# Eleven transfers of six partitions in place of half a block of wo

## The chip, the cores and the metric

The kernel runs on one core of a Trainium2 chip. The metric is device time in microseconds (us) of one execution. All inputs lie in the chip's memory (HBM) and are brought by DMA into SBUF, which has 128 partitions; a core's DMAs are carried by 16 DMA engines, told apart from the compute engines TensorE (PE; PEld for its weight loads), VectorE (DVE), ScalarE (ACT), GpSimd (POOL) and SyncE (SP). SP computes nothing here: it issues nearly all DMAs.

## The reference, cut to what matters

One decode step of a transformer block: attention over a key and a value cache, and a small MLP. B = 4 sequences, one new token each, H = 32 heads, Sk = 4096 cached positions, Dh = 128, D = 640, F = 1728, all bfloat16.

```python
q = (layernorm(x) @ wq)                     # (4, 640) @ (640, 4096), split into 32 heads
scores = einsum("bhqd,bhkd->bhqk", q, k_cache) * Dh ** -0.5
p = softmax(scores)
o = einsum("bhqk,bhkd->bhqd", p, v_cache)
h = x + o.reshape(4, 4096) @ wo             # wo: (4096, 640)
out = h + mlp(layernorm(h))                 # (640, 1728), an activation, (1728, 640)
```

The two caches have 4 * 32 * 4096 * 128 elements each, 134.2 MB; wo has 5.2 MB.

## The kernel before, in words

**Groups.** The 32 heads and 4 sequences are walked in NG = 32 groups, `g = 0..31`: a group is G = 4 heads (`hq = g // 4`) of one sequence (`b = g % 4`). The key tile `kt` of a group is `[128, 128, 128]`: a partition holds 128 positions of one head, 32 KB, so that 128 partitions hold four heads of 4096 positions. One DMA of 4 MB brings it; `vt`, the value tile, is alike. There are two buffers of each.

**A group's work.** DVE multiplies `kt` by the broadcast query (line 367, in four parts), PE sums over the head's dimension by matmuls with the identity (line 374), DVE ends that sum (line 386), the softmax follows (lines 393 to 425), and in the next group PE multiplies the probabilities by `vt` (line 257).

**Order of the DMAs.** It is written out by hand (`manual_schedule`): instructions run on each engine in the order of the program, and every DMA but the load of x goes through SP. At the end of group `g` SP issues `kt` of group g + 2 (when the buffer that group g used is free), then `vt` of group g + 1. In groups 8 to 11, after these two, it issues two blocks of wo each. The loads that follow the last group's are those of the MLP's weights (lines 501 to 507). The last `vt` (group 31) comes in four quarters, the last `kt` in two halves.

**wo.** The tile `wo_sb` is `[128, 32, 640]`; a block is 4 of its 32 rows `h`, 640 KB, 128 partitions with 5120 contiguous bytes each (in the last block, four times 1280 bytes). The eight blocks are read by `project(hq)` (line 344), block `hq` by `project(hq)`, at the end of groups 14, 15, 16, 17, 22, 26 and 30 (`PROJ_AT`) and once after the loop. Block 5, which is `h = 20..23`, is read in group 26. `wo_sb` takes the memory that wq had.

**What the prediction's steps touch.** `load_kv` (line 92; DMAs at line 100), the loop over groups (line 427), the loads of wo (line 471), the load of b1 (line 476, one partition), the load of x (line 110, four partitions, by ACT), the store of the output (line 649, 20 partitions), `pv_moving` (line 254).

The calls of lines 449 to 474, with the diff, show the order in which a group ends:

```python
        if g + 2 < NG:
            kts[g + 2] = load_k(g + 2)
        if 1 <= g < NG - 1:
            pv_moving(g - 1, 0, R)
            pv_copy(g - 1)
            vts.pop(g - 1)
        if g in PROJ_AT:
            project(PROJ_AT[g])
        if g + 1 < NG:
            vts[g + 1] = load_v(g + 1)
        ...
        if g in WO_AT:
            ...
```

Of the kernel before, what the change touches and what calls it, by code (L numbers as in the profile page):

```python
# [16 lines left out]
def kernel(  # L17
# [24 lines left out]
    nc = tc.nc  # L42

    B, Sq, D = A_x.shape
    _, H, Sk, Dh = A_k_cache.shape
# [3 lines left out]
    G = 4  # L49
# [5 lines left out]
    HQ = H // G  # L55
# [47 lines left out]
    def load_k(g):  # L103
        return load_kv(kpool, "kt", A_k_cache, g, NP)

    def load_v(g):
        return load_kv(vpool, "vt", A_v_cache, g, VP)
# [35 lines left out]
    for q in range(G):  # L143
        nc.vector.tensor_copy(
            out=sel[:, :, q, q * PH : (q + 1) * PH],
            in_=ident[0:N, 0:N].unsqueeze(2).to_broadcast([N, N, PH]),
# [81 lines left out]
    for hq in Q_AT[-1]:  # L228
# [12 lines left out]
        out=pick[:, :],  # L241
        in_=ident_f[:, :].rearrange("p (t i) -> p i t", t=T)[:, 0 : J * G, :],
# [11 lines left out]
    def pv_moving(g, r0, r1):  # L254
        for r in range(r0, r1, J):
            c0 = 128 // T * (r // J % T)
            nc.tensor.matmul(  # L257
                p_ps[c0 : c0 + J * G, :],
                lhsT=e2[g % NE2][:, r : r + J, :].rearrange("p j q -> p (j q)"),
                rhs=vts[g][:, r : r + J, :].rearrange("p j d -> p (j d)"),  # L260
                start=(r < J * T),
                stop=(r >= r1 - J * T),
            )

    def pv_copy(g):
        blocks[g] = work.tile([128, J * Dh], FP32, tag="p_sb", bufs=1, name=f"p_sb{g}")
        nc.scalar.copy(out=blocks[g][:, :], in_=p_ps[:, :])  # L267

    def add_blocks(g, stop=True):
        o = ot_of(g)  # L270
        p_sb = blocks.pop(g)
        for j in range(J):
            nc.tensor.matmul(  # L273
                o,
                lhsT=p_sb[:, j * Dh : (j + 1) * Dh],
                rhs=pick[:, j * G : (j + 1) * G],
                start=(j == 0),
                stop=(stop and j == J - 1),
            )
        return o  # L280
# [13 lines left out]
    def row_sums(hq):  # L294
        l_ps = ps.tile([128, N, G], FP32, tag="small")
        nc.tensor.matmul(  # L296
            l_ps[:, :, :],
            lhsT=ones_f[:, :],
            rhs=rs2[:, hq * N : (hq + 1) * N, :],
            start=True,  # L300
            stop=True,
        )
        rls[hq] = work.tile([128, N, G], FP32, tag="rl", name=f"rl{hq}")
        nc.vector.reciprocal(out=rls[hq][:, :, :], in_=l_ps[:, :, :])  # L304

    def normalise(hq):
        nc.vector.tensor_tensor(
            out=otn[:, hq, :, :],
            in0=ot.pop(hq)[:, :, :],
            in1=rls.pop(hq)[:, :, :],  # L310
            op=ALU.mult,
        )
# [15 lines left out]
    def regroup(hq):  # L328
        o4_ps = ps.tile([128, G, N], FP32, tag="small", name=f"o4_{hq}")
        for q in range(G):  # L330
            for i in range(G):
                nc.tensor.matmul(  # L332
                    o4_ps[q * PH : (q + 1) * PH, i, :],
                    lhsT=ident4[:, i, :],
                    rhs=otn[:, hq, :, q],
                    start=True,
                    stop=True,
                )
        nc.scalar.copy(out=o4[:, hq, :, :], in_=o4_ps[:, :, :])

    yT = ps.tile([128, DC, N], FP32, tag="yT")
    wo_sb = []

    def project(hq):

        for h in range(hq * G, (hq + 1) * G):
            for c in range(DC):
                nc.tensor.matmul(
                    yT[:, c, :],
                    lhsT=wo_sb[0][:, h, c * 128 : (c + 1) * 128],  # L350
                    rhs=o4[:, hq, h % G, :] if hq < HQ - 1 else otn[:, hq, :, h % G],
                    start=(h == 0 and c == 0),
                    stop=(h == H - 1 and c == DC - 1),
                )
# [3 lines left out]
    def mul_and_sum(g, part):  # L358

        hq, b = divmod(g, N)  # L360
        r0 = part * RP
        kt = kts[g][:, r0 : r0 + RP, :]
        s_ps = ps.tile([128, RP, W], FP32, tag="s", bufs=2, name=f"s{g}_{part}")
        s_of[g, part] = s_ps
        for k in range(NQ):
            d0 = k * DQ
            nc.vector.tensor_tensor(  # L367
                out=kt[:, :, d0 : d0 + DQ],
                in0=kt[:, :, d0 : d0 + DQ],
                in1=qbs[:, hq, b, d0 : d0 + DQ].unsqueeze(1).to_broadcast([128, RP, DQ]),  # L370
                op=ALU.mult,
            )
            for d in range(d0, d0 + DQ, W):
                nc.tensor.matmul(  # L374
                    s_ps[:, :, :],
                    lhsT=ident[:, :],
                    rhs=kt[:, :, d : d + W],
                    start=(d == 0),
                    stop=(d == Dh - W),
                )  # L380
            yield

    def finish_sum(g, part):
        if part == 0:
            s_sbs[g] = work.tile([128, R], FP32, tag="s_sb", name=f"s_sb{g}")
        nc.vector.tensor_reduce(  # L386
            out=s_sbs[g][:, part * RP : (part + 1) * RP],
            in_=s_of.pop((g, part))[:, :, :],
            axis=AX.X,
            op=ALU.add,  # L390
        )
# [35 lines left out]
    for g in range(NG):  # L427
        hq, b = divmod(g, N)
        for part in range(NP):
            now = mul_and_sum(g, part)  # L430
            before = None
            next(now)
            if part > 0:
                finish_sum(g, part - 1)
                if g >= 2:
                    add_blocks(g - 2)
                    if b == 1:
                        row_sums(hq - 1)
                        normalise(hq - 1)
                if g in PROJ_AT:  # L440
                    regroup(PROJ_AT[g])
            elif g >= 1:
                finish_sum(g - 1, NP - 1)
                before = softmax(g - 1)
                next(before)
            next(now)
            if before is not None:
                next(before)
        kts.pop(g)
# [10 lines that stand above are left out]
        for n in Q_AT.get(g, ()):  # L460
            q_chunk(n)
            q_broadcast(n)
        if g in WO_AT:

            if not wo_sb:
                wo_sb.append(wbig.tile([128, H, D], BF16, tag="w", name="wo_sb"))
            h0 = WO_AT[g] * WOC
            for h in range(h0, h0 + WOC, G):

                order = "(p i) n -> p i n" if h + G < H else "(i p) n -> p i n"  # L470
                nc.sync.dma_start(
                    out=wo_sb[0][:, h : h + G, :],
                    in_=A_wo[h * Dh : (h + G) * Dh, :].rearrange(order, i=G),
                )
            if WO_AT[g] == 0:
                nc.sync.dma_start(out=b1_row[:, :], in_=B_b1.rearrange("(o f) -> o f", o=1))
        if g == B1_AT:
            b_ps = ps.tile([128, FC], FP32, tag="small", name="b_ps")
            for c in range(FC):
                cols, fw = f_chunk(b1_row[:, :], c)  # L480
                nc.tensor.matmul(
                    b_ps[0:fw, c : c + 1],
                    lhsT=cols,
                    rhs=ident[0:1, 0:1],
                    start=True,
                    stop=True,
                )
            nc.vector.tensor_copy(out=b1T[:, 0:C2], in_=b_ps[:, 0:C2])
            nc.vector.tensor_copy(out=b1T[0:FREM, C2:FC], in_=b_ps[0:FREM, C2:FC])
# [56 lines left out]
    for dst in (h2T, hc):  # L546
        nc.vector.tensor_tensor(
            out=dst[:, :, :],
# [10 lines left out]
    for c0, c1 in W1_PARTS:  # L559
        for c in (0, C2, *range(1, C2)):  # L560
# [9 lines left out]
            if c0 == 0 and c == 4:  # L570
# [3 lines left out]
                    out=std[:, :], in_=v_ps[:, :], func=ACT.Sqrt, bias=eps_t[:, :], scale=1.0  # L574
# [5 lines left out]
        out=h1n[:, :, :],  # L580
# [6 lines left out]
        out=h1s[:, :, :],  # L587
# [9 lines left out]
        out=tb[:, :, :],  # L597
# [8 lines left out]
        out=ta[:, :, :], in0=tb[:, :, :], scalar1=-0.5, scalar2=-1.0, op0=ALU.mult, op1=ALU.add  # L606
# [4 lines left out]
        out=act_t[:, :, :],  # L611
# [10 lines left out]
    for i, (w2, c) in enumerate(w2_of):  # L622
        rows = 128 if c < C2 else FREM
# [10 lines left out]
        out=oT[:, :, :].rearrange("p n c -> p c n"),  # L634
# [46 lines left out]
```

## Time and profile before

| what | value |
|---|---|
| median of three runs | 667.99 us (667.97 to 668.5) |
| the profiled execution's own time | 668.62 us |
| its span, first to last instruction | 666.8 us |
| bytes moved by DMA | 283.81 MB, mean 426 GB/s |
| share of the 16 DMA engines' time that the data's queue took | 98.9% |
| busy: PE, DVE, ACT, POOL | 444.7, 353.4, 115.0, 2.4 us |
| mean granted TensorE clock | 0.837 of full speed |

The profile is of one execution. The span leaves out 1.8 us of that execution's time, which lie before the first and after the last instruction, and the execution took 0.63 us longer than the median of the runs. A queue's share is the time that its packets took, as a share of the time of 16 DMA engines over the span. A packet is what one DMA engine moves in one piece; here it is one partition's contiguous bytes, 32768 in a `kt` or `vt`. The trace keeps of each packet its queue, start, duration and size, but not which of the 16 DMA engines carried it.

### The profile page before, as it was taken

What the parts mean: (1) busy time and instruction counts of PE and PEld (TensorE: products, weight loads), DVE (VectorE), ACT (ScalarE), POOL (GpSimd) and SP (SyncE); (2) the same over time, 40 slices, a digit from 0 to 9 for tenths busy, and PEclk for the clock granted to TensorE, in tenths of its full rate; (3) what the DMA queues carried; (4) which work ended last, traced back from release to release, by engine and by line L of the source; (5) the groups of instructions that cost most, each with busy time, mean ns of one, the idle gap of its engine ahead of it and who ended that gap; (6) DMA issues with size and microseconds to landing.
All of it is one profiled execution on the core that took longest, in us unless ns stands there. A gap on an engine that the chain in (4) does not pass through costs nothing.

```text
span 666.8 us, 7101 instructions
## 1 busy us (share of the span) xinstructions
PE 444.7 (67%) x3081; PEld 202.7 (30%) x3081; DVE 353.4 (53%) x306; ACT 115.0 (17%) x352; POOL 2.4 (0%) x13
## 2 busy tenths in 40 slices
PE   0588777887666485388666757757657785665876
PEld 0233333343222232133323323322223332222335
DVE  2485544566655366246654545656444666455732
ACT  0022122131101111011101111111011121011132
POOL 1000000000000000000000000000000000000000
PEclk9997889797779876777778898777798797779995
DMA  9999999999999999999999999999999999999996
GB/s 376 436 435 425 431 440 431 426 431 438 433 427 433 429 439 420 442 430 426 432 434 433 428 429 437 436 431 425 437 435 432 424 436 437 431 431 428 438 412 247
DMA packets 12871, 283.81 MB, mean 426 GB/s; under 512 B 1379, under 2 KB 2087, under 8 KB 4008
## 3 DMA queue, kind: packets, MB, share of 16 engines
q1 hardware_dynamic: 12832, 283.36, 98.9%
q8 instruction: 24, 0.39, 0.2%
q14 instruction: 7, 0.06, 0.0%
q10 hardware_dynamic: 8, 0.01, 0.0%
HBM read 283.35 MB, written 0.01 MB: 425 GB/s over the span
## 4 chain that ended last, share of the span: by engine, by line
DMA 62%; PE 21%; DVE 15%; issue 1%; ACT 0%; SPq 0%; DVEq 0%; ACTq 0%
DMA kt<-in_A_k_cache_dram 59%; PE s L374 16%; DVE kt L367 13%; DMA vt<-in_A_v_cache_dram 3%; DVE s_sb L386 1%; PE ot L273 1%; PE tr L399 1%; PE p_ps L257 1%; PE h_ps L563 0%; DVE mx L404 0%; PE q_ps L195 0%; PE y2T L625 0%; PE qb_ps L209 0%; PE tr L412 0%; PE o L332 0%
## 5 line engine op out<-in xcount | busy, mean ns | idle before, releaser
L374 PE MATMUL s<-kt,ident 128*128 128x512 bf16 x1024 | 300.0, 446 | 190.1 <-DVE kt L367 187.9
L367 DVE TENSOR_TENSOR kt<-kt,qbs 128x4096 bf16<-128x4096 bf16 x128 | 291.5, 2279 | 234.2 <-DMA kt<-in_A_k_cache_dram 234.2
L374 PEld LDWEIGHTS <-ident 128*128 128x128 bf16 x1024 | 109.4, 110 | 337.4 <-issue 170.6
L417 ACT ACTIVATE e<-s_sb,nbs 32x128 bf16<-32x128 f32 x128 | 74.0, 578 | 2.5
L257 PE MATMUL p_ps<-vt,e 128*16 128x512 bf16 x1016 | 63.4, 392 | 1.4 <-DMA vt<-in_A_v_cache_dram 1.4
L414 ACT COPY nbs<-tr 128x4 f32<-128x4 f32 x32 | 5.2, 162 | 332.0 <-PE tr L412 332.0
L386 DVE TENSOR_REDUCE s_sb<-s 128x64 f32<-128x512 f32 x64 | 43.6, 681 | 4.7 <-PE s L374 4.5
L267 ACT COPY p_sb<-p_ps 128x512 f32<-128x512 f32 x32 | 18.7, 585 | 151.8 <-PE p_ps L257 151.7
L273 PEld LDWEIGHTS ot<-pick,p_sb 128*128 128x128 f32 x256 | 34.3, 196 | 6.3 <-ACT p_sb L267 2.0
L257 PEld LDWEIGHTS <-e 128*16 128x16 bf16 x1016 | 23.0, 90 | 39.7 <-issue 19.0
L417 ACT ACTIVATION_READ_ACCUMULATOR e<-s_sb,nbs 32x1 f32 x128 | 32.2, 252 | 0.0
L273 PE MATMUL ot<-pick,p_sb 128*128 128x4 f32 x256 | 31.4, 246 | 1.0 <-ACT p_sb L267 1.0
L404 DVE TENSOR_REDUCE mx<-tr 1x4 f32<-1x128 f32 x32 | 8.9, 278 | 25.6 <-PE tr L399 25.5
L195 PE MATMUL q_ps<-wq_sb,xT 128*4 128x512 bf16 x40 | 11.0, 409 | 9.8 <-DMA wq_sb<-in_A_wq_dram 9.8
L399 PE MATMUL tr<-ident_f,pm 128*1 128x128 f32 x64 | 16.0, 345 | 1.2 <-DVE pm L397 1.2
L412 PEld LDWEIGHTS tr<-mx,nscale 1*128 1x128 f32 x64 | 9.4, 182 | 13.8 <-issue 11.4
L304 DVE RECIPROCAL rl<-l_ps 128x16 f32<-128x16 f32 x8 | 2.1, 258 | 20.3 <-PE l_ps L296 20.3
L209 PE MATMUL qb_ps<-q_all,sel 4*128 4x128 bf16 x128 | 9.2, 225 | 5.3 <-ACT q_all L202 5.3
L412 PE MATMUL tr<-mx,nscale 1*128 1x4 f32 x64 | 12.2, 258 | 0.4 <-DVE mx L404 0.4
L209 PEld LDWEIGHTS <-sel 4*128 4x128 bf16 x128 | 8.4, 98 | 9.1 <-issue 9.1
L202 ACT CAST q_all<-q_ps 4x512 bf16<-4x512 f32 x8 | 4.6, 574 | 35.0 <-PE q_ps L195 35.0
L399 PEld LDWEIGHTS tr<-ident_f,pm 128*1 128x1 f32 x64 | 2.8, 81 | 24.7 <-issue 24.7
(85 smaller groups left out, 75.2 us busy)
## 6 DMA issues: line engine op xcount, KB each, us to landing
kt<-in_A_k_cache_dram SPq DMA_DIRECT2D x31, 4096.0 KB, 25.1
vt<-in_A_v_cache_dram SPq DMA_DIRECT2D x31, 4096.0 KB, 33.3
wq_sb<-in_A_wq_dram SPq DMA_DIRECT2D x1, 5120.0 KB
wo_sb<-in_A_wo_dram SPq DMA_DIRECT2D x8, 640.0 KB, 35.6
kt<-in_A_k_cache_dram SPq DMA_DIRECT2D x2, 2048.0 KB
vt<-in_A_v_cache_dram SPq DMA_DIRECT2D x4, 1024.0 KB, 18.6
w<-in_B_w_dram SPq DMA_DIRECT2D x3, 640.0 KB, 17.8
w<-in_B_w_dram SPq DMA_DIRECT2D x1, 1296.0 KB, 25.3
```

Of the source, the lines that this page charges most:

```text
L195: nc.tensor.matmul(q_ps[:, :], lhsT=xT[:, c, :], rhs=wq_sb[:, c, n * QC : (n + 1) * QC], start=(c == 0), stop=(c == DC - 1),)
L209: nc.tensor.matmul(qb_ps[:, b * Dh : (b + 1) * Dh], lhsT=sel[:, b, q, :], rhs=q_all[:, h * Dh : (h + 1) * Dh], start=(q == 0), stop=(q == ...
L257: nc.tensor.matmul(p_ps[c0 : c0 + J * G, :], lhsT=e2[g % NE2][:, r : r + J, :].rearrange("p j q -> p (j q)"), rhs=vts[g][:, r : r + J, :]. ...
L267: nc.scalar.copy(out=blocks[g][:, :], in_=p_ps[:, :])
L273: nc.tensor.matmul(o, lhsT=p_sb[:, j * Dh : (j + 1) * Dh], rhs=pick[:, j * G : (j + 1) * G], start=(j == 0), stop=(stop and j == J - 1),)
L367: nc.vector.tensor_tensor(out=kt[:, :, d0 : d0 + DQ], in0=kt[:, :, d0 : d0 + DQ], in1=qbs[:, hq, b, d0 : d0 + DQ].unsqueeze(1).to_broadcas ...
L374: nc.tensor.matmul(s_ps[:, :, :], lhsT=ident[:, :], rhs=kt[:, :, d : d + W], start=(d == 0), stop=(d == Dh - W),)
L386: nc.vector.tensor_reduce(out=s_sbs[g][:, part * RP : (part + 1) * RP], in_=s_of.pop((g, part))[:, :, :], axis=AX.X, op=ALU.add,)
L399: nc.tensor.matmul(tr_ps[0:1, 0:128], lhsT=pm[:, :], rhs=ident_f[:, :], start=True, stop=True)
L404: nc.vector.tensor_reduce(out=mx[:, :], in_=tr_ps[0:1, 0:128].rearrange("o (a b) -> o a b", a=G), axis=AX.X, op=ALU.max,)
L412: nc.tensor.matmul(nb_ps, lhsT=nscale[:, :], rhs=mx[:, :], start=True, stop=True)
L417: nc.scalar.activation(out=e2[g % NE2][p0:p1, :, q], in_=s_sb[p0:p1, :], func=ACT.Exp, bias=nb[p0:p1, q : q + 1], scale=SCALE, accum_out=r ...
```

## The change

Of block 5 of wo (`H_FEW = 20`) the one transfer in group 10 now brings only the 64 even partitions. The 64 odd partitions come in eleven transfers, one as the last DMA of each of groups 12 to 22. Transfer i brings the partitions 1 + 2i, 23 + 2i, 45 + 2i, and so on, 22 apart: six of them for i = 0 to 8, five for i = 9 and 10. A partition still has 5120 contiguous bytes. All else stays.

```diff
+    H_FEW = H - 3 * G
+    FEW_AT = {HQ + 4 + i: i for i in range(11)}
+    few_rows = []
+
+    def load_few(p0, step, n):
+        part = slice(p0, p0 + step * (n - 1) + 1, step)
+        nc.sync.dma_start(
+            out=wo_sb[0][part, H_FEW : H_FEW + G, :], in_=few_rows[0][part, :, :]
+        )
...
-                nc.sync.dma_start(
-                    out=wo_sb[0][:, h : h + G, :],
-                    in_=A_wo[h * Dh : (h + G) * Dh, :].rearrange(order, i=G),
-                )
+                rows = A_wo[h * Dh : (h + G) * Dh, :].rearrange(order, i=G)
+                if h != H_FEW:
+                    nc.sync.dma_start(out=wo_sb[0][:, h : h + G, :], in_=rows)
+                else:
+                    few_rows.append(rows)
+                    load_few(0, 2, 64)
             if WO_AT[g] == 0:
                 nc.sync.dma_start(out=b1_row[:, :], in_=B_b1.rearrange("(o f) -> o f", o=1))
+        if g in FEW_AT:
+            load_few(1 + 2 * FEW_AT[g], 22, 6 if FEW_AT[g] < 9 else 5)
```

## The prediction

> **What bounds the kernel now.** I read the page first: its shares of the span, the DMA slices, the queues and the chain.
>
> ```profile
> span 666.8 us, 7101 instructions
> DMA  9999999999999999999999999999999999999996
> DMA packets 12871, 283.81 MB, mean 426 GB/s; under 512 B 1379, under 2 KB 2087, under 8 KB 4008
> q1 hardware_dynamic: 12832, 283.36, 98.9%
> q8 instruction: 24, 0.39, 0.2%
> q14 instruction: 7, 0.06, 0.0%
> DMA 62%; PE 21%; DVE 15%; issue 1%; ACT 0%; SPq 0%; DVEq 0%; ACTq 0%
> ```
>
> All 16 DMA engines are busy until the last slice. Beside the data's queue q1, queues q8 and q14 bring instructions, little in bytes. The table by stretches (PE, PEld, DVE, ACT, POOL busy, then clock, DMA share, GB/s) says how full the engines are:
>
> ```profile
> 40.00:300.00 260.00, 179.84 (x1132) 79.59 (x1131) 137.18 (x108) 48.68 (x144) 0.00 (x0) 0.82 1.00 432
> 300.00:500.00 200.00, 133.71 (x961) 60.10 (x962) 110.83 (x90) 32.17 (x106) 0.00 (x0) 0.83 1.00 432
> ```
>
> A share of 1.00 at 432 GB/s, 27.0 GB/s an engine: an engine that loses a microsecond cannot make it up. The end of the chain says which loss counts:
>
> ```profile
> 628.77 20.61 DMA vt<-in_A_v_cache_dram
> 649.39 0.04 issue
> 649.43 1.05 PE p_ps L257 x7
> ```
>
> Seven matmuls wait for the third quarter of the last vt; then 17.4 us of short dependent steps lead to the end at 666.8. A load has landed when the last of 16 engines has its part, so what counts is the latest engine.
>
> The trace doesn't name a packet's engine, but a packet starts some 3 ns before its engine's last one ends, so I joined packet records, end to start, into 16 chains. Between 2 us and the last quarter of vt I found no gap above 25 ns (one chain, 644.87 below, is lost after 530 us and carried on with its lag). A 32768-byte packet follows every 1.21 us (took 1213 ns), a 5120-byte one every 0.193 (took 196), a completion of 4 bytes adds 0.006. Each 16384-byte packet of q8 sets its chain back by 1.42 for good; they go round eight chains, 22 of them before the third quarter lands. The 8192-byte packets of q14 cost about 0.84 each, on other chains. The third quarter's landing in the 16 chains, us:
>
> ```
> eight chains with q8:  647.46 647.87 648.70 648.79 648.83 648.92 648.95 649.10
> the eight others:      644.37 644.73 644.87 645.09 645.10 645.64 646.05 647.02
> ```
>
> The early half waits 2 to 5 us for the late half. Which are the six engines of a six-partition transfer? By their completions, the output's 20 partitions took ten engines, x's four took four, b1's one took one: six and five rows should take six and five. x's four chains are those at 644.37, 644.87, 646.05 and 647.02, and b1's is one of them (644.87): small transfers begin with the same engines, all early. I call them engines 0 to 3; engines 4 and 5 are not to be seen.
>
> **The change, part by part.** SP issues 11 more DMAs, 0.33 to 0.43 us each by its rows, 4.7 us in all: hidden, because in groups 12 to 22 SP stands for some 18 us a group until DVE has used a kt. A new DMA may have to wait for the one before it, since both write the same rows of the tile. It would land just after the vt issued before it, about 33 us after issue (median of vt), so SP could stand 13 us. Behind it in SP's queue is only the next kt, issued 12 to 26 us later; and at those issues the earliest chain still had 7.3 to 19.3 us of queued packets. Cost 0; without that cover each us beyond the slack would be a us. Block 5 is read in group 26, near 549 us; its last rows are issued near 472 and land near 506: no wait, 0. Reads of other blocks use other columns; that such reads need not wait is seen at the MLP, whose first matmuls start at 656.19 while later columns of their tile land until 661.5. Some extra waits on PE that are long over: under 1 us once, beneath waits of 9 us for kt.
>
> On the DMA engines the half block takes 4 packets from each where the block took 8: -4 x 0.193 = -0.77 us for each. Engines 0 to 4 get 11 packets back: 11 x 0.193 + 11 x 0.006 = +2.19, net +1.42; engine 5 nine, net +1.02. Alone, that lowers the late half to 649.10 - 0.77 = 648.33 and lifts the latest known early engine to 647.02 + 1.42 = 648.44, a gain of 0.66 us.
>
> The unknown is what a packet costs that goes to another engine's partitions. A load of 128 partitions gives each engine 8. A few-partition transfer gives engine j the row 1 + 2i + 22j, across the whole width, so nearly every one of the 64 packets enters partitions into which another engine is pouring kt at full pace, and so may half of the even rows. No row of before shows that: all large loads have 128 partitions. Bounds: at the low end such a packet takes 0.193 and disturbs nobody. At the high end it goes like the only small packets here that met another stream, the 5120-byte ones beside a q8 fetch on one engine: 538 and 548 ns for 196. Nothing speaks for less than 0.193. Between them I take equal sharing, 2 x 0.193 = 0.386 for the packet and 0.193 lost by the disturbed engine, because wherever two streams meet in this trace the packet lengthens and the delay stays in its chain to the end. Then, for the engine at 647.02:
>
> removed -8 x 0.193 = -1.54; half block 4 x 0.193 = +0.77; eleven packets 11 x 0.386 = +4.25; their completions +0.07; four packets of others into its own partitions (64 over 16) 4 x 0.193 = +0.77. Sum +4.32, landing 651.34.
>
> The late half saves 0.77 and is disturbed by four packets, +0.77: still 649.10. So the third quarter lands 651.34 - 649.10 = 2.2 us later; the 17.4 us behind it stay. The profiled execution would go from 668.62 to 670.8, the median from 667.99 to 670.2.
>
> The Trainium skill (SBUF — State Buffer, section "Door 1: The DMA port swizzle") speaks against the change: the DMA side has 16 ports, each serving eight fixed partitions at 27.2 GB/s, however many engines write to them. By that rule the loads' 27.0 GB/s an engine leave a port no room and the sum is the +2.2; were engines alone the limit it would be the -0.66. No row here can show two engines at one port.
>
> With the half block's even rows disturbed too, add up to 0.77: +3.0. With 0.538 for each of the eleven, 5.92 for 4.25: +3.9. If the engine at 646.05 were the latest: +1.3.
>
> **The rivals.** A change of 0.2%, 1.34 us, is about what a measurement can tell from none.
>
> First rival, not slower: packets don't disturb each other, and the DMA engines alone count. For it: all chains keep the same pace whatever lies beside them. Against it: nothing in the trace tests it. Price -0.66: 667.3. It decides wherever a foreign packet costs its engine under about 0.23 and its neighbour under 0.05 us.
>
> Second rival, partial disturbance: 0.23 to 0.32 a packet, and what exceeds 0.193 lost by the neighbour, -0.1 to +1.3: 667.9 to 669.3, within 0.2%.
>
> Third rival: engine 4 or 5 is in the late half. Undisturbed 649.10 + 1.42: 669.4; with sharing 649.10 + 4.32: 672.3. Against it: all four engines that can be named are early.
>
> Fourth: the eleven waits of SP let the queue run dry. Each us past a slack of 7.3 is a us; a stall of 10 in one group gives 670.7. Against it, the slack in every other such group is above 8.
>
> Fifth: the eleven are spread over all engines, or the bytes move with no effect on the latest: 668.0.
>
> **How the numbers follow.** Sharing as summed, 0.46: 670.2 (its own range 669.3 to 671.9). Undisturbed 0.25, partial 0.12, late engine 0.08, no effect 0.04, queue dry 0.02, something faster that I don't see 0.03. Slower by over 0.2%: 0.46 + 0.08 + 0.02 = 0.56. Within: 0.25 + 0.12 + 0.04 = 0.41. Faster: 0.03, as no engine is relieved of more than 0.77 us. The range, 667.0 to 671.9, holds the first rival's 667.3 with the runs' spread of some 0.3, and the sum with 0.538 a packet.
>
> **What the changed profile would show.** Sharing: 5120-byte packets between 270 and 510 us well above 196 ns, 32768-byte ones beside them above 1213, and the third quarter's landing in the end chain near 651.6 instead of 649.4, with the steps behind it unchanged. Undisturbed: all at 196 and 1213, landing near 648.7. The DMA share between 300 and 500 us stays 1.00; SP's waits may gain some for DMA wo_sb without a change of the kt waits in the chain. I am wrong if the packets keep their lengths and the time still grows, or if the share falls below 1.00.

## The result and the profile after

The changed kernel takes 671.06 us (median of five runs, 670.98 to 672.01) where the kernel before takes 668.50 (five runs, 667.97 to 668.78): +2.56 us. The ratio is 1.0040, its 95% interval 1.0029 to 1.0052. The profiled execution took 671.04 us, its span 669.2: 2.42 more than the one before, 2.4 of it inside the span. Of the page, the span, the DMA slices, the queues and the chain's shares:

```profile
span 669.2 us, 7114 instructions
DMA  9999999999999999999999999999999999999995
DMA packets 12935, 283.81 MB, mean 424 GB/s; under 512 B 1443, under 2 KB 2151, under 8 KB 4072
q1 hardware_dynamic: 12896, 283.36, 98.7%
DMA 62%; PE 19%; DVE 17%; issue 1%; ACT 0%; SPq 0%; DVEq 0%; ACTq 0%
```

The same bytes, in 64 more packets, which are the 4-byte completions of the eleven transfers, one for each row; the even half has 16, as the block had, and the 5120-byte packets are as many as before. The table by stretches (PE, PEld, DVE, ACT, POOL busy, then clock, DMA share, GB/s):

```profile
40.00:300.00 260.00, 181.59 (x1142) 80.36 (x1141) 136.69 (x107) 49.00 (x145) 0.00 (x0) 0.82 1.00 432
300.00:500.00 200.00, 132.54 (x946) 59.59 (x946) 110.12 (x88) 31.62 (x106) 0.00 (x0) 0.82 1.00 429
```

Up to 300 us nothing has changed: 432 GB/s. Between 300 and 500, where the small transfers are, the engines are still never idle (share 1.00), but move 429 GB/s instead of 432. So each was always at work on a packet and some packets took longer. The end of the chain of waits:

```profile
630.59 21.06 DMA vt<-in_A_v_cache_dram
651.70 1.06 PE p_ps L257 x8
```

The third quarter lands at 630.59 + 21.06 = 651.65 us, before at 649.39: +2.26. From there to the end of the span it is 17.5 us, before 17.4. Nearly the whole loss is in the landing.

The packets show it one by one. I call "added length" the time by which the 32768-byte packets that start between 205 and 585 us exceed 1213 ns, summed over all 16 engines, less the same sum of before (7.5 us, all from packets beside instruction fetches). It is 21.9 us, 1.37 for each engine. Between 250 and 600 us 413 of 4507 packets lie between 1225 and 1400 ns; before, none. They stand in ten clusters of 1.5 to 2.7 us in all, each at one of the last ten small transfers; beside the first, in group 12, there is nothing. Packets of nearly every engine are lengthened, by some 50 ns each in the mean. The 5120-byte packets of the small transfers themselves take 199 ns in the mean, at most 221. Some packets of the cluster in group 14 (start in us, length in ns, bytes; others that start between them are left out):

```
346.372   196   5120
346.413   196   5120
346.461  1249  32768
346.535  1259  32768
346.761  1353  32768
347.122   196   5120
347.280  1359  32768
347.393  1296  32768
347.489  1321  32768
```

The third quarter's 16 completions, in us, are to be compared with the two rows of the prediction:

```
645.32 645.59 645.95 647.15 647.21 647.86 648.03 648.15
648.68 649.34 649.49 649.58 649.65 649.66 650.17 651.30
```

Five of the late ones come at 649.3 to 649.7, one at 650.17, and the last stands alone at 651.30, 1.1 us after all others. In the chains it is the one that carries nine small packets, not eleven, hence the sixth of a small transfer, engine 5; its lag behind the first packet of a transfer grows by 1.63 us between the transfers at 327 and 346 us, where q8 fetches 16384 bytes at 333. Engines 0 to 4 show no such step at a q8 fetch. The one at 650.17 has q14 fetches at 372 and 642 us, as the chain at 647.02 had at 373 and 639 before the change.

On SP the new DMAs take longer to issue than other loads of wo. The instructions of the tile wo_sb (ns min/median/max):

```profile
L350 SPq DMA_DIRECT2D wo_sb<-in_A_wo_dram x12: 559/704/5240, 226.1 to 473.3; - x12
L484 SPq DMA_DIRECT2D wo_sb<-in_A_wo_dram x7: 422/424/426, 187.7 to 249.4; - x7
```

and SP's and DVE's longest sums of waiting, from the tables of waits, first before and then after the change:

```profile
SPq L100 <- DVE kt L367: 469.5, 30, 34.1
DVE kt L367 <- DMA kt<-in_A_k_cache_dram: 234.2, 31, 18.5
```

```profile
SPq L100 <- DVE kt L378: 458.0, 30, 33.7
DVE kt L378 <- DMA kt<-in_A_k_cache_dram: 237.9, 31, 18.2
```

SP stood 469.5 us for used kt tiles before and 458.0 now, so the added issues came out of its slack, and no wait for wo_sb is among the waits. DVE's waiting for kt grew from 234.2 to 237.9 us.

### The profile page after: what moved, and what is told of

It is laid out like the page before. It is cut to its first block, busy times and chain, and to the rows that moved or that the text cites. A ratio compares the mean times of both kernels' runs of the same rounds, so it can differ in the third digit from the quotient of the medians.

```text
span 669.2 us, 7114 instructions
## 1 busy us (share of the span) xinstructions
PE 448.0 (67%) x3081; PEld 203.7 (30%) x3081; DVE 353.2 (53%) x306; ACT 115.0 (17%) x352; POOL 2.4 (0%) x13
## 4 chain that ended last, share of the span: by engine, by line
DMA 62%; PE 19%; DVE 17%; issue 1%; ACT 0%; SPq 0%; DVEq 0%; ACTq 0%
DMA kt<-in_A_k_cache_dram 59%; PE s L385 14%; DVE kt L378 14%; DMA vt<-in_A_v_cache_dram 3%; DVE s_sb L397 1%; PE ot L273 1%; PE tr L410 1%; PE p_ps L257 1%; DVE mx L415 1%; PE h_ps L578 0%; PE q_ps L195 0%; PE y2T L640 0%; PE qb_ps L209 0%; PE o L332 0%; ACT q_all L202 0%
## 5 line engine op out<-in xcount | busy, mean ns | idle before, releaser
L378 DVE TENSOR_TENSOR kt<-kt,qbs 128x4096 bf16<-128x4096 bf16 x128 | 291.5, 2280 | 237.9 <-DMA kt<-in_A_k_cache_dram 237.9
L257 PE MATMUL p_ps<-vt,e 128*16 128x512 bf16 x1016 | 66.5, 407 | 1.4 <-DMA vt<-in_A_v_cache_dram 1.4
```

The lines of the kernel that those rows point to most:

```text
L257: nc.tensor.matmul(p_ps[c0 : c0 + J * G, :], lhsT=e2[g % NE2][:, r : r + J, :].rearrange("p j q -> p (j q)"), rhs=vts[g][:, r : r + J, :]. ...
L378: nc.vector.tensor_tensor(out=kt[:, :, d0 : d0 + DQ], in0=kt[:, :, d0 : d0 + DQ], in1=qbs[:, hq, b, d0 : d0 + DQ].unsqueeze(1).to_broadcas ...
```

## The experiments

The theory after the result: a row that a DMA engine writes into partitions of another engine costs time in the load packets (**place**), and the engine that ends last is the sixth, which has instruction fetches too (**engine 5**). Rivals: the eleven extra transfers cost by being small and separate, wherever they write (**transfers**); the even half costs too; the order of rows in HBM does it.

**e1_five: no row for engine 5.** Thirteen transfers of five rows (the last of four), 26 partitions apart.

```diff
-    FEW_AT = {HQ + 4 + i: i for i in range(11)}
+    FEW_AT = {HQ + 4 + i: i for i in range(13)}
-            load_few(1 + 2 * FEW_AT[g], 22, 6 if FEW_AT[g] < 9 else 5)
+            load_few(1 + 2 * FEW_AT[g], 26, 5 if FEW_AT[g] < 12 else 4)
```

> The 64 odd partitions come in 13 transfers of five partitions, 26 apart (the last of four), in groups 12 to 24, so that only engines 0 to 4 carry them; the 64 even ones in group 10 as in the changed kernel. Theory A (engine 5 has instruction fetches, is the latest, and carries nine packets more; beside that all 32768-byte packets near a small transfer lengthen, 1.33 us an engine in all): engine 5 is relieved like the others, the late half stands at 649.10 - 0.77 + 1.33 = 649.7, the latest of engines 0 to 3 at 647.02 - 0.77 + 13 x 0.199 + 1.33 = 650.2, so the third quarter lands 1.1 us later than before: about 669.1 for 668.0. Theory B (sharing as in the prediction, engines 0 to 3 the latest): 13 packets for 11 at 0.386 each, 3.0 us later than before, 671.0.

Measured: 670.16 us against 668.52, ratio 1.0031 (1.0022 to 1.0041). The end of the chain of waits:

```profile
629.37 21.17 DMA vt<-in_A_v_cache_dram
650.59 1.05 PE p_ps L257 x7
```

It lands at 650.54, 1.11 us before that of the change, though the added length is no smaller, 23.8 us. The landing is 1.15 us later than before, as expected (1.1); the time is 1.64 later. So without a row for engine 5 the end comes about 1.1 us of the 2.26 earlier; what is left is the lengthening that all engines share and the thirteen rows of the engine that is the latest now. By the terms found here that would be the engine that was at 647.02: -1.54 + 0.77 + 13 x 0.199 + 23.8 / 16 = +3.31, 650.3. The last completion comes at 650.16, in a chain with thirteen small packets and with q14 fetches at 372 and 640 us.

**e2_halves: only the halving.** The 64 odd partitions in one transfer in group 12.

```diff
-    FEW_AT = {HQ + 4 + i: i for i in range(11)}
+    FEW_AT = {HQ + 4: 0}
-            load_few(1 + 2 * FEW_AT[g], 22, 6 if FEW_AT[g] < 9 else 5)
+            load_few(1, 2, 64)
```

> The block comes in two transfers of 64 partitions, the even ones in group 10 and the odd ones in group 12, 16 engines each. Theory A: each engine has eight packets of the block as before and no small transfer passes: no 32768-byte packet lengthened, time within 0.2 us of before. Theory B, with half of each engine's rows in other engines' partitions: up to 8 x 0.193 = 1.5 us later, and 5120-byte packets above 196 ns.

Measured: 668.58 against 668.52, ratio 1.0002 (0.9992 to 1.0011); added length 0.1 us, and the end of the chain of waits as before:

```profile
628.24 21.11 DMA vt<-in_A_v_cache_dram
649.39 1.06 PE p_ps L257 x7
```

A transfer of 64 alternate partitions on 16 engines costs what it moves and no more. All of the loss belongs to the eleven. The trace doesn't show which engine carries which of the 64 rows, so whether these lie in other engines' partitions and are free all the same, or lie in their own, stays open.

**e3_extra22 and e4_extra4: the same eleven, two places.** Both are the kernel before, with eleven extra transfers that bring rows of block 5 once more, with the values that they have. In e3_extra22 they are the rows of the change, 22 apart:

```diff
+        if 12 <= g <= 22:
+            i = g - 12
+            p0, step, n = 1 + 2 * i, 22, (6 if i < 9 else 5)
+            part = slice(p0, p0 + step * (n - 1) + 1, step)
+            nc.sync.dma_start(
+                out=wo_sb[0][part, 20:24, :],
+                in_=A_wo[20 * Dh : 24 * Dh, :].rearrange("(p i) n -> p i n", i=G)[part, :, :],
+            )
```

In e4_extra4 they are six rows four apart, from partitions 0 to 3 and 32 to 35 in turn:

```diff
-            p0, step, n = 1 + 2 * i, 22, (6 if i < 9 else 5)
+            p0, step, n = i % 4 + 32 * (i // 4 % 2), 4, 6
```

> The kernel before, all 128 partitions in one transfer, and beside that the changed kernel's eleven transfers once more, which write the same values again. Theory A: engine 5 has nine packets more, 9 x 0.199 = 1.79, and the lengthening, 1.33: 3.1 us later than before, 671.1. Theory B: 647.02 + 11 x 0.386 + 0.07 + 0.77 = 652.1 for 649.1, 3.0 us later. The two agree here: this is the base for the run with rows four apart.

> As the run with the extra transfers, but the eleven transfers of six partitions bring rows c, c + 4, ..., c + 20 (c = 0 to 3 and 32 to 35), so that engine j writes partitions that it writes in the large loads too, if those are dealt out four by four. If the lengthening comes from writing other engines' partitions: no 32768-byte packet above some 1225 ns except beside a fetch, and engine 5 alone makes the time, 11 x 0.199 = 2.2 us later than before, 670.2. If small transfers lengthen the others wherever they go: 2.2 + 1.33 = 3.5 us, 671.5. Theory B, which has engines 0 to 3 as the latest: 647.02 + 2.19 = 649.2, 0.1 us later.

Measured: e3_extra22 671.79 against 668.52, ratio 1.0049 (1.0034 to 1.0064), added length 23.8 us; e4_extra4 670.32, ratio 1.0028 (1.0017 to 1.0039), added length 0.1 us. The ends of the chains, e3_extra22 first:

```profile
631.91 20.72 DMA vt<-in_A_v_cache_dram
652.67 1.05 PE p_ps L257 x7
```

```profile
627.89 17.01 DMA vt<-in_A_v_cache_dram
644.91 19.20 DMA w<-in_B_w_dram
664.11 0.05 issue
664.16 1.16 PE y2T L633 x30
```

Nearly as many packets (64 and 66) of the same size, in as many transfers in the same groups, lengthen the loads by 23.8 us in one place and by 0.1 in the other. That rules out "transfers". It also agrees with the rule of the Trainium skill (SBUF — State Buffer, section "Door 1: The DMA port swizzle") that partitions four apart lie at different ports, with partitions p and p + 32 at the same one, and that in a full-width load the engines 0 to 7 serve the ports of partitions 0 to 31 in order, four partitions each. By that e4_extra4's rows go where their own engine writes anyway. But its rows also lie close together, within 21 partitions, and e3_extra22's across the whole width. No run has several rows close together in other engines' partitions, so for such transfers the two aren't told apart; only e11_one, below, has a single row in one such place. e3_extra22's landing, +3.24, is engine 5's nine rows, 9 x 0.199 = 1.79, and 23.8 / 16 = 1.49: +3.28. In e4_extra4 next to nothing is lengthened and it is still 1.8 us longer. Its end is set by the weights of the MLP (w), landing at 664.11: a q8 fetch at 656 us comes after the third quarter (PE's wait for that ends at 649.86) but ahead of the last of w. By the lags of the small packets it lies on engine 5, which has eleven rows more; the chains are not certain there, and which of the eight has which fetch differs between executions. Whether engine 5 alone makes the 1.8 is tested next.

**e9_own5: e4_extra4 with five rows,** so without engine 5:

```diff
-            p0, step, n = i % 4 + 32 * (i // 4 % 2), 4, 6
+            p0, step, n = i % 4 + 32 * (i // 4 % 2), 4, 5
```

> The extra transfers four apart once more, but of five partitions instead of six, so that engine 5 carries none of them. If engine 5 and its instruction fetches make the end: the latest of engines 0 to 4 comes to 647.02 + 11 x 0.199 = 649.2, the late half stays at 649.1, so the time is within 0.3 us of before. If a small transfer costs the end something by itself, whoever carries it: about 1.7 us later, as with six partitions.

Measured: 668.94 against 668.58, ratio 1.0005 (0.9996 to 1.0015), added length 0.0. The end of the chain of waits, within 0.15 us of before:

```profile
628.24 21.26 DMA vt<-in_A_v_cache_dram
649.54 1.05 PE p_ps L257 x8
```

Fifty-five extra rows on engines 0 to 4 are nearly free; the eleven of engine 5 were what made e4_extra4 slow. Engine 5 is in the late half.

**e6_src22, e7_dst22: HBM or SBUF.** e4_extra4 again (but five rows in the last two transfers), with source and destination apart: e6_src22 writes rows four apart from HBM rows 22 apart, e7_dst22 the reverse.

```diff
+            s0, sstep, _ = 1 + 2 * i, 22, (6 if i < 9 else 5)                       # e6_src22
+            s0, sstep, _ = i % 4 + 32 * (i // 4 % 2), 4, (6 if i < 9 else 5)        # e7_dst22
```

> Extra transfers whose rows in SBUF are four apart, as in the run without lengthening, but whose rows in HBM are the changed kernel's, 22 apart; block 5 of wo then holds some wrong rows. If the place in SBUF makes the lengthening: none, below 0.2 us in all. If the place in HBM makes it: about 21 us summed over the engines.

> The other way round: rows in SBUF 22 apart as in the changed kernel, rows in HBM four apart, some wrong rows in block 5 again. Place in SBUF: about 21 us of lengthening summed over the 16 engines. Place in HBM: none.

Measured, one run each: e6_src22 670.30, added length 0.0 us; e7_dst22 671.64, 23.9 us; before 668.66. The stretch of the small transfers in e6_src22 and then in e7_dst22:

```profile
300.00:500.00 200.00, 133.67 (x946) 59.67 (x947) 110.56 (x87) 31.56 (x105) 0.00 (x0) 0.80 1.00 432
```

```profile
300.00:500.00 200.00, 132.06 (x944) 59.31 (x945) 109.22 (x86) 31.55 (x105) 0.00 (x0) 0.85 1.00 428
```

432 GB/s against 428: the place in SBUF makes the loss, the rows read do not.

**e8_sixteen: sixteen rows at a time.** The odd rows in four transfers of 16 partitions, eight apart, in groups 12 to 15: four rows for each engine, as in one transfer of 64.

```diff
-    FEW_AT = {HQ + 4 + i: i for i in range(11)}
+    FEW_AT = {HQ + 4 + i: i for i in range(4)}
-            load_few(1 + 2 * FEW_AT[g], 22, 6 if FEW_AT[g] < 9 else 5)
+            load_few(1 + 2 * FEW_AT[g], 8, 16)
```

> The 64 odd partitions in four transfers of 16, eight apart, in groups 12 to 15, one row for each engine. Each engine carries eight rows of the block, as before, but 14 of 16 engines write a row that lies in another engine's partitions. If a row in another engine's partitions costs all engines some 0.02 us: 64 rows, about 1.2 us later than before, 669.7, and 32768-byte packets lengthened by about 19 us in all. If what costs is only the unequal load of the engines: 0 within 0.2 us.

Measured: 670.64 against 668.66, ratio 1.0031 (1.0019 to 1.0044), +2.0 us: more than I expected. The added length is 26.8 us, and the small packets themselves take 1.0 us more (up to 300 ns): 27.8 / 16 = 1.74 us for each engine. The completions of the load that lands near 590 us are later by 1.66 in the mean, which is that. No engine has more rows than before here, so this run shows the disturbance alone: spread over 16 engines it moved the end by 2.0. It is 0.43 us a row, in packets of up to 1.68 us (1213 ns without).

**e5_same: always the same six rows,** partitions 1, 23, 45, 67, 89 and 111, eleven times (the insert of e3_extra22 with `p0, step, n = 1, 22, 6`). **e10_from13: the change one group later,** `FEW_AT = {HQ + 5 + i: i for i in range(11)}`. Both ask why the first small transfer of the change lengthened nothing.

> The kernel before and eleven extra transfers in groups 12 to 22, all of the rows 1, 23, 45, 67, 89, 111, written again with the same values. In the changed kernel the transfer of these rows, the first of the eleven, was the only one beside which no 32768-byte packet lengthened. If it is these rows that disturb nobody: no packet above 1225 ns beside any of the eleven. If it is that the first such transfer is always free: about 2.1 us of lengthening, summed over the 16 engines, beside each of the ten others, 21 us in all.

> The changed kernel with its eleven transfers in groups 13 to 23 instead of 12 to 22. In the changed kernel the one of group 12 had no lengthened packets beside it. If the first one is free whenever it comes: none beside that of group 13, some 2 us summed over the engines beside each of the ten others. If it is the place in the run: lengthening beside all eleven. The time in both cases some 2.5 us above before, 671.

Measured, one run each: e5_same 671.84 against 668.66, added length 19.0 us, none beside the transfer of group 12 and some 2 us beside each of the ten others. e10_from13 671.76 against 668.58, 21.4 us in ten clusters, none beside its first transfer, now in group 13. So it is neither the rows nor the time: the first one is free.

**e11_one: one row at a time; e12_ownfirst: an own-port transfer first.** Again the insert of e3_extra22, with

```diff
-            p0, step, n = 1 + 2 * i, 22, (6 if i < 9 else 5)
+            p0, step, n = 64, 1, 1                                                   # e11_one
+            p0, step, n = (1 + 2 * i, 22, (6 if i < 9 else 5)) if i else (0, 4, 5)   # e12_ownfirst
```

> The kernel before with eleven extra transfers in groups 12 to 22, each of one row only: partition 64 of block 5 again, with its own values. Per row (each row written into another engine's partitions costs the 16 engines some 0.35 to 0.40 us in all, the first transfer nothing): 32768-byte packets lengthened by 3.5 to 4 us in all, 0.25 an engine; time +0.2 to +0.6. Per transfer (each few-row transfer into other engines' partitions costs some 2.1 us in all, whatever its rows): 21 us in all, 1.3 an engine; time +1.3 to +1.7. One engine alone carries the eleven rows, +2.2 us; if it is the one whose part landed at 647.02, that alone lifts it to 649.3.

> The kernel before with eleven extra transfers: the first, in group 12, of five rows four apart, the ten others as the change has them, 22 apart. If the first small transfer of any kind is free: all ten beside lengthened packets, 21 to 24 us in all, the cluster of group 13 too. If the first one into other engines' partitions is free: nine clusters, 19 to 21 us, none beside the transfer of group 13. Time 671 to 672 in both.

Measured: e11_one 668.77 against 668.65, ratio 1.0001 (0.9991 to 1.0010). The added length is 1.3 us: neither the 3.5 to 4 of a price by the row nor the 21 of one by the transfer. Each small packet takes 196 ns, and one load packet beside it, in each of the last nine transfers, is longer by 0.13 to 0.14 us; beside the second transfer one by 0.075, beside the first none. The first three that lengthened a packet and the last (end of the small packet, then start of the lengthened one relative to it, and its excess, us):

```
327.67   -0.12   0.075
347.23   -0.24   0.139
366.79   -0.30   0.132
503.72   -0.72   0.136
```

(In the profiled execution the chain of waits at the end doesn't hold the third quarter, and the chain with the eleven rows lands it at 646.66, ahead of nine others.) Here is nearly the picture that the prediction had: one engine, one neighbour, one packet that pays. It also suggests why the first was free in this run: shifted back by the row's 0.199 us, the neighbour's next packet began 0.08 us after the small one had ended (a packet starts at 308.187, the small one ends at 308.105), so the row fell into the last 0.3 us of a neighbour's packet and cost it nothing; the second overlapped the next packet by 0.12 and cost half.

e12_ownfirst took 671.87 in its one run, added length 24.3 us, more than the 19 to 21 expected: none beside the five rows four apart of group 12, 0.3 beside the first six-row transfer 22 apart, in group 13, and 1.7 to 3.7 beside each of the nine others. So it isn't any first small transfer that is free, but the first with rows 22 apart, into other engines' partitions. Whether the phase seen in e11_one explains this for six rows at once the runs don't settle.

The runs side by side. "Rows" are those written 22, 26 or 8 apart or alone, less those of the first transfer where that was free; "landing" is the third quarter's in the chain, where it is in it (before 649.39).

| kernel | time against before, us | added length, us | rows | us a row | landing |
|---|---|---|---|---|---|
| the change | +2.56 | 21.9 | 58 | 0.38 | 651.65 |
| e1_five | +1.64 | 23.8 | 59 | 0.40 | 650.54 |
| e2_halves | +0.06 | 0.1 | | | 649.35 |
| e3_extra22 | +3.27 | 23.8 | 58 | 0.41 | 652.63 |
| e4_extra4 | +1.80 | 0.1 | | | |
| e9_own5 | +0.36 | 0.0 | | | 649.50 |
| e8_sixteen | +1.98 | 26.8 | 64 | 0.42 | |
| e11_one | +0.12 | 1.3 | 10 | 0.13 | |

One row alone costs others 0.13 us; five to sixteen at once cost 0.38 to 0.42 each, spread thinly over all engines. Why they cost three times as much together, and reach engines into whose partitions few of them can go, stays open.

No version here beats the kernel before, and the prices say that moving rows off late engines in this way won't: a row taken from a late engine saves it 0.193 us, and given to another engine in a group of five or more it costs each of the 16 some 0.4 / 16 = 0.025. The late half is eight engines, so lowering all of them by one row takes eight rows, 8 x 0.025 = 0.2 against 0.193. That is worked out, not run.

## Why the prediction was right, point by point

**What sets the end: right.** The third quarter of the last vt stayed the wait that counts, and the time went with its landing: +2.26 of the +2.4 in the span, with 17.5 us behind it.

**SP and the tile's waits at nothing: right in the sum, wrong in the price.** A six-row DMA took 0.70 us to issue, not 0.33 to 0.43, the first 5.24; all of it came out of SP's slack. DMA share 1.00, no dry queue: the fourth rival is out.

**Even half undisturbed: right.** e2_halves gives +0.06 us, so the 0.77 that the forecast kept for its upper end isn't there.

**Six and five rows on six and five engines: right.** The small packets come six and five at a time, at the lags of six and five chains. The fifth rival, the eleven spread over all engines, is out.

**The price of a row into foreign partitions: right in all, wrong in how it falls.** This is one of the two steps that failed. The prediction took 0.386 us for the packet and 0.193 lost by the disturbed engine, which is 0.193 + 0.193 = 0.386 of added time a row. Measured are 0.38 a row of added time, but the small packet takes 199 ns and the whole of the loss lies in load packets, of nearly all 16 engines alike. So the first sign, "5120-byte packets between 270 and 510 us well above 196 ns", did not come; the second, 32768-byte ones above 1213, and the third, a landing near 651.6, did. For an engine of the first five the sum is not +4.32 but -1.54 + 0.77 + 11 x 0.199 + 1.37 = +2.79: the one at 647.02 would be at 649.8, not 651.34 (seen at 650.17, if its q14 fetches tell it rightly). The late half is not held at 649.10 by -0.77 + 0.77; it is at -0.77 + 1.37 = +0.60, 649.7, as seen (five completions at 649.3 to 649.7).

**The latest engine: wrong.** This is the other step. It isn't the early one at 647.02 but engine 5, which "is not to be seen" in the trace of before and belongs to the late half: the third rival's condition, given 0.08. With nine packets, -1.54 + 0.77 + 9 x 0.199 + 1.37 = +2.39 from one of the late completions near 648.9 gives 651.3, as seen. e1_five and e9_own5 show it: without a row for engine 5 the landing is 1.1 us earlier, and eleven own-port transfers lose 0.36 instead of 1.80. The third rival's own prices (669.4 undisturbed, 672.3 with sharing) missed on both sides, since it put eleven packets on the engine and either no disturbance or the whole of it there.

**So the forecast's +2.2 and the measured +2.4 in one execution agree by two errors that cancel, which is luck.** The prediction laid 4.25 - 2.12 = 2.13 us of lengthening and 0.77 of disturbance on an engine that had 2 us to spare; the chip laid 1.37 on all of them, and the one that counted had no time to spare. The first rival, undisturbed, would have been slower too: engine 5 alone, -0.77 + 1.79, makes +1.0.

**The rule cited against the change.** By the Trainium skill (SBUF — State Buffer, section "Door 1: The DMA port swizzle") each port serves eight fixed partitions at a fixed rate. Taken strictly, a second writer then costs the first. e11_one agrees in kind (a packet longer by 0.135 us for a row that takes 0.196), and so do the rows four apart, which cost nobody anything. The rule alone doesn't give what six rows together do: they lengthen packets of nearly all engines, by 0.38 us a row in all.

## What to carry to other kernels

In a kernel whose DMA engines are full, count engines, not bytes: join the packets into chains, see which engines are late and why (here the instruction fetches of 1.42 us), and expect a transfer of k < 16 rows to go to the same k engines each time, one of which may be late. Mind where a few-row transfer writes when it lies beside a full-width load: five or six rows four partitions apart, from 0 to 3 or 32 to 35, lengthened nothing, while rows 22, 26 or 8 apart cost the loads some 0.4 us of engine time a row. Halving a block by alternate partitions, still on 16 engines, was free.

## What the runs showed of the hardware that was not expected

- Five to sixteen 5120-byte rows written at once 22, 26 or 8 partitions apart lengthen the 32768-byte packets of nearly all 16 engines, 1213 ns to some 1220 to 1420 (up to 1682 with sixteen rows), 0.38 to 0.42 us a row in all. A single row lengthens one packet by 0.13 to 0.14 us. The short packets of the change hardly lengthen: 199 ns for 196.
- A row that falls into the last 0.3 us of the neighbour's packet cost it nothing (e11_one's first), and the first few-row transfer into other engines' partitions cost next to nothing in eight of the kernels (the change, e1_five, e3_extra22, e5_same, e7_dst22, e10_from13, e11_one, e12_ownfirst: 0.0 to 0.3 us); with sixteen rows the first cost as well.
- SP took 0.70 us to issue a DMA of six rows (the first 5.24), 0.42 for one of 128.
- The 16384-byte instruction fetches of q8 fall on eight of the 16 DMA engines, 1.42 us each; the sixth engine of a small transfer is one of them, the first five aren't. The 8192-byte ones of q14 fall on others and cost 0.55 to 0.84 us each (0.84 for each in the prediction; before the change three of the five after 300 us cost 0.55 to 0.59).
